# Second token block's output product in plain form, weight sums on VectorE instead of GpSimd, denser activation steps in the last turn

## The chip, the cores and the metric

The kernel runs on one core of one Trainium2 chip. The metric is device time in microseconds (us), lower is better. Verdicts use a margin of 2%. The engines are TensorE (PE in the profile; PEld is its weight load), VectorE (DVE), ScalarE (ACT), GpSimd (POOL) and SyncE (SP). PSUM is the memory in which TensorE's products are formed and from which VectorE or ScalarE takes them here; SBUF is the on-chip memory of the other operands. The granted clock is the share of TensorE's full clock that the profile shows. "TensorE stands" means that it is idle. One matmul of the program shows in the trace as two records; counts such as x5777 are records.

## The reference

A gated recurrence over 4 x 8 heads of 768 tokens with head size 48 gives a 3072 x 384 matrix; a feed-forward layer with the activation h * erf(softplus(h)) follows.

```python
f = 1.0 / (1.0 + np.exp(-f_logit))
for t in range(S):
    state = f[:, :, t, :, None] * state + np.einsum('bhd,bhe->bhde', k[:, :, t], v[:, :, t])
    y[:, :, t] = np.einsum('bhd,bhde->bhe', q[:, :, t], state)
x = y.transpose(0, 2, 1, 3).reshape(B * S, H * D)     # 3072 x 384
h = x @ w_in                                          # 384 -> 2048
g = h * erf(np.maximum(h, 0.0) + np.log1p(np.exp(-np.abs(h))))
return g @ w_out                                      # 2048 -> 384
```

## The kernel before

The 3072 tokens form 12 blocks of 256. The main loop has 12 turns (`it` from 0 to 11). In one turn TensorE works through a list of slots, one matmul each: the hidden product (`x @ w_in`) of one block and the output product (`g @ w_out`) of an earlier one. Between slots come the steps of the recurrence (`stage_d`, `stage_t`, `stage_s`, `stage_y`), the steps of the activation (`act_step`) and the steps of the block sums (`sum_step`). The program order on each engine is the order in which this loop emits the instructions.

The output product of a block comes in two forms. The plain one, `project_first`, was used for block 0 alone. The other, `project`, splits the matrices into 2 x 2 blocks and needs seven products of half size instead of eight. For that, VectorE must form sums of the hidden values (`sum_h`, 16 instructions a block), sums of `w_out` must have been formed once (`sum_w`, 16 instructions), and VectorE has to combine the seven products as they leave PSUM (`plus`).

```python
def activate(gr):                       # one group: 4 x 256 hidden values on 128 partitions
    e = epool.tile(...)                 # two buffers
    exp(e, h)                           # ScalarE, line 157
    yield
    for i in range(n):
        term(xs[i], h, i)               # ScalarE tanh, line 160; may load its table first
        yield
    for i in range(n):
        times(e, xs[i], i)              # VectorE, line 165
        yield
    ...
    nc.scalar.activation(out=e[:], in_=e[:], func=AF.Tanh, scale=SERF_C)      # line 559
    yield
    nc.vector.tensor_tensor(out=h, in0=h, in1=e[:], op=ALU.mult)              # line 561
    gr["done"] = True
...
def sum_w(gi):
    ...
    add(t[:, 0], b12, b11, ALU.subtract, nc.gpsimd)      # line 615, on GpSimd
    yield
    ... # three more
def sum_h(gr):
    while not gr["done"]:
        act_step()                      # line 636: steps forced, beside those placed by the slots
    ... # four adds on VectorE, line 615
def project_first(blk):
    ...  # the same `while` before each of the
         # 2 x 4 matmuls 128x384 per group, line 670; then
                    if j == FG - 1 and tt == CPB - 1:
                        to_sum.append(sum_w(gi))
...
def project(blk):
    ...  # matmuls 128x192, line 717 (718 in the changed kernel)
    def plus(out, x, y):                # line 725 (726 in the changed kernel)
        nc.vector.tensor_tensor(out=out, in0=x, in1=y, op=ALU.add)
    ...
def slots(it):
    ...
    if it == 2:
        return chain(*hiddens(3), project_first(0)), n_h + n_ft * CPB
    if it < n_blocks - 1:
        return chain(project(it - 2), *hiddens(it + 1)), n_o + n_h
    return chain(*[project(blk) for blk in range(n_blocks - 3, n_blocks)]), 3 * n_o
```

In the recurrence, `stage_d` is the decay product (TensorE, line 380), then two exponentials on ScalarE (`dp`, line 383, and `kd`, line 386), then two products on VectorE (`qd`, line 395, and line 399). `stage_y` is the product `y` (line 525). It writes into one of the two PSUM buffers that the transposes of `stage_t` also use, so it has to wait until the copy of `kT` (VectorE, line 422) has emptied one.

## Time and profile before

| | before |
|---|---|
| time, median of 4 runs with the changed kernel in the same rounds | 629.17 us (628.93 to 629.83) |
| span of the profiled run | 627.6 us |
| TensorE busy | 589.5 us, 94% |
| VectorE busy | 470.2 us, 75% |
| GpSimd busy | 38.4 us, 6% |
| waits of TensorE after 160 us | 5.9 + 3.8 + 1.1 + 1.0 + 0.4 us |

The table is read from the last row up: TensorE is the engine that must not stand, and after 160 us it stands for 12.2 us in five places (the sum of the last row). What GpSimd did at that time is seen in the groups of instructions of the kernel before, cut to GpSimd (line, engine, operation, names, shapes and count; then busy time and the mean of one in ns):

```profile
L615 POOL TENSOR_TENSOR wT<-w_out_sb 128x384 f32<-128x384 f32 x8 | 12.2, 1524 | 0.0
L615 POOL TENSOR_TENSOR wT<-w_out_sb,wT 128x384 f32<-128x384 f32 x8 | 11.2, 1396 | 3.8 <-PE ops L670 3.6
```

These 16 sums are 23.4 of GpSimd's 38.4 us. They are the part of the change that moves. (The program reuses its buffers, so names such as `wT`, `scratch` and `kn` in the views can also hold hidden values or sums.)

### The profile page before, as it was taken

The numbers are of one execution on the slowest core, as the hardware profiler recorded it, in microseconds if no ns is written. First come the engines' busy times: TensorE is split into PE (matmuls) and PEld (weight loads), VectorE is DVE, ScalarE is ACT, GpSimd is POOL, SyncE is SP. The second block draws the span as 40 slices with busy tenths as digits, with TensorE's granted clock in tenths as the row PEclk, the third lists the DMA queues.
The fourth block names the chain that finished last, engine by engine and source line by source line (L and its number), as shares of the span: only waits on it lengthen the run. The fifth ranks groups of instructions, "written<-read, shape, count | busy, mean of one in ns | idle before, by whom it ended". The sixth has DMA issues, their size and how long they took to land.

```text
span 627.6 us, 13891 instructions
## 1 busy us (share of the span) xinstructions
PE 589.5 (94%) x5777; PEld 524.7 (84%) x5777; DVE 470.2 (75%) x788; ACT 382.4 (61%) x483; POOL 38.4 (6%) x49
## 2 busy tenths in 40 slices
PE   8788699998976999999999999999999999999995
PEld 7567588887644988988998998998998989989995
DVE  4998998695589778678787876797887694756751
ACT  5725457978864457756675776765775656556200
POOL 1000011010176000000000000000000000000000
PEclk9879799999989899999999999999999999999999
DMA  9997743440321043043052052052030000000000
GB/s 200 247 241 215 216 123 63 88 78 12 63 56 26 1 78 76 1 79 75 4 102 52 2 102 51 3 102 52 3 76 14 2 27 1 19 8 1 25 26 29
DMA packets 155587, 41.35 MB, mean 66 GB/s; under 512 B 147328, under 2 KB 150400, under 8 KB 155520
## 3 DMA queue, kind: packets, MB, share of 16 engines
q1 hardware_dynamic: 153440, 40.02, 29.3%
q8 instruction: 47, 0.77, 0.5%
q10 hardware_dynamic: 2080, 0.39, 0.3%
q14 instruction: 20, 0.16, 0.1%
HBM read 35.59 MB, written 4.72 MB: 64 GB/s over the span
## 4 chain that ended last, share of the span: by engine, by line
PE 72%; DVE 12%; issue 6%; ACT 5%; DMA 2%; SPq 1%; POOL 1%; DVEq 0%; ACTq 0%; POOLq 0%
PE ops L717 31%; PE hps L587 29%; PE y L525 3%; PE ps_t L411 2%; PE ops L670 2%; PE ps_d L380 2%; DVE sv L438 1%; PE sc L460 1%; PE sc L468 1%; DVE sv L439 1%; DVE w_in_sb L322 1%; DMA qn<-in_q_dram 1%; DVE qA L496 1%; DVE w_in_sb L336 1%; ACT L160 1%
## 5 line engine op out<-in xcount | busy, mean ns | idle before, releaser
L587 PE MATMUL hps<-xT,w_in_sb 128*128 128x256 f32 x1152 | 264.7, 386 | 7.8 <-DVE w_in_sb L336 4.4
L587 PEld LDWEIGHTS hps<-xT,w_in_sb 128*128 128x128 f32 x1152 | 218.2, 192 | 41.2 <-DVE w_in_sb L336 3.4
L165 DVE SCALAR_TENSOR_TENSOR e<-x,e 128x1024 f32<-128x1024 f32 x96 | 120.2, 1252 | 13.5 <-ACT x L160 13.2
L160 ACT ACTIVATE x<-Hg,serf_bias 128x1024 f32<-128x1024 f32 x88 | 97.6, 1141 | 0.2
L157 ACT ACTIVATE e<-Hg 128x1024 f32<-128x1024 f32 x44 | 46.6, 1058 | 77.0 <-DVE Hg L561 73.2
L717 PE MATMUL ops<-wT,Hg 128*128 128x192 f32 x352 | 87.6, 331 | 0.0
L717 PE MATMUL ops<-wT,scratch 128*128 128x192 f32 x320 | 76.5, 331 | 5.9 <-DVE scratch L615 5.9
L717 PE MATMUL ops<-w_out_sb,Hg 128*128 128x192 f32 x352 | 72.6, 329 | 0.0
L561 DVE TENSOR_TENSOR Hg<-Hg,e 128x1024 f32<-128x1024 f32 x44 | 54.6, 1240 | 22.5 <-ACT e L559 22.4
L717 PEld LDWEIGHTS ops<-wT,Hg 128*128 128x128 f32 x352 | 62.1, 192 | 2.2
L594 ACT COPY Hg<-hps 128x1024 f32<-128x1024 f32 x44 | 44.4, 1010 | 31.0 <-PE hps L587 30.7
L717 PEld LDWEIGHTS ops<-w_out_sb,Hg 128*128 128x128 f32 x352 | 60.7, 192 | 2.6
L717 PEld LDWEIGHTS ops<-wT,scratch 128*128 128x128 f32 x320 | 57.0, 193 | 6.2 <-issue 6.2
L559 ACT ACTIVATE e<-e 128x1024 f32<-128x1024 f32 x48 | 50.4, 1050 | 6.4 <-DVE e L165 6.3
L496 DVE TENSOR_TENSOR qA<-sc,tri 64x256 f32<-64x256 f32 x68 | 28.7, 422 | 22.3 <-PE sc L468 21.3
L725 DVE TENSOR_TENSOR scratch<-scratch,ops 128x384 f32<-128x384 f32 (+1 forms) x44 | 22.2, 504 | 30.3 <-ACT scratch L733 25.0
L418 ACT COPY qA<-ps_t 64x512 f32<-64x512 f32 x48 | 27.7, 578 | 22.5 <-PE ps_t L411 20.6
L395 DVE TENSOR_TENSOR qd<-qn,dp 128x384 f32<-128x384 f32 x24 | 13.4, 556 | 35.6 <-ACT dp L383 34.4
L717 PE MATMUL ops<-w_out_sb,scratch 128*128 128x192 f32 x160 | 39.5, 328 | 0.0
L525 PEld LDWEIGHTS y<-qA,sv 128*32 128x32 f32 x1536 | 24.6, 113 | 17.2 <-issue 9.2
L525 PE MATMUL y<-qA,sv 128*32 128x64 f32 x1536 | 28.9, 226 | 9.3 <-issue 6.9
L438 DVE TENSOR_TENSOR sv<-sc,sv 48x192 f32<-48x192 f32 x80 | 28.4, 354 | 8.3 <-ACT qA L488 6.9
(109 smaller groups left out, 648.9 us busy)
## 6 DMA issues: line engine op xcount, KB each, us to landing
lt<-in_f_logit_dram SPq DMA_DIRECT2D x24, 192.0 KB, 3.8
qn<-in_q_dram SPq DMA_DIRECT2D x24, 192.0 KB, 3.3
out_dram<-scratch SPq DMA_DIRECT2D x12, 384.0 KB, 2.6
kn<-in_k_dram SPq DMA_DIRECT2D x23, 192.0 KB, 3.5
vt<-in_v_dram SPq DMA_DIRECT2D x23, 192.0 KB, 3.6
sv<-in_v_dram SPq DMA_DIRECT2D x84, 48.0 KB, 2.9
w_out_sb<-in_moe_w_in_dram SPq DMA_DIRECT2D x4, 768.0 KB, 6.3
Hg<-in_moe_w_in_dram SPq DMA_DIRECT2D x4, 768.0 KB, 6.4
```

Source lines behind the costliest of these rows:

```text
L157: nc.scalar.activation(out=dst[:], in_=h, func=AF.Exp)
L160: nc.scalar.activation(out=dst[:], in_=h, func=AF.Tanh, bias=serf_bias[:, i : i + 1], scale=SERF_KAB[i][0])
L165: nc.vector.scalar_tensor_tensor(out=e[:], in0=x[:], scalar=SERF_KAB[i][2], in1=e[:], op0=ALU.add, op1=ALU.mult)
L418: nc.scalar.copy(out=qAs[g][half(r), r], in_=pss[0][half(r)])
L438: nc.vector.tensor_tensor(out=new, in0=add, in1=old, op=ALU.add)
L496: nc.vector.tensor_tensor(out=qA[half(1 - r), r, :, half(c)], in0=sc[half(c), r], in1=tri1[half(c)].unsqueeze(1).broadcast_to((C, HP, C)), ...
L525: nc.tensor.matmul(y[M * i : M * (i + 1), kt, half(c)], lhsT=sv[:, r, c, a, o : o + M], rhs=qA[:, r, a, half(c)], start=(n == 0), stop=Tru ...
L559: nc.scalar.activation(out=e[:], in_=e[:], func=AF.Tanh, scale=SERF_C)
L561: nc.vector.tensor_tensor(out=h, in0=h, in1=e[:], op=ALU.mult)
L587: nc.tensor.matmul(hps[:, j, :], lhsT=w_in_sb[:, kt, ft * P : (ft + 1) * P], rhs=xTs[blk][:, kt, :], start=(kt == 0), stop=(kt == n_k - 1),)
L594: nc.scalar.copy(out=gr["h"], in_=hps[:])
L717: nc.tensor.matmul(place[n], lhsT=x[:, j, :], rhs=y, start=(gi == 0 and j == 0 and n in first), stop=(gi == n_g - 1 and j == 1), skip_grou ...
```

## The change

The intent: block 1's product becomes plain, so that it needs no block sums and cannot wait for them. `w_out`'s sums, now needed one turn later, go to VectorE, spread over every second slot of turns 2 and 3. The activation steps get a new spacing in turn 3 and a closer one in the last turn. The core of the diff, cut:

```diff
-        add(t[:, 0], b12, b11, ALU.subtract, nc.gpsimd)
+        add(t[:, 0], b12, b11, ALU.subtract)
 ... (the same for the other three)
-                        to_sum.append(sum_w(gi))
+                        if blk == 0:
+                            to_sum.append(sum_w(gi))
 ...
+        if it == 3:
+            return chain(project_first(1), *hiddens(4)), n_ft * CPB + n_h
 ...
-                at = ([0] if it + 2 == ADJACENT else []) + [2, 26, 42, 54, 76, 90]
+                at = [0, 1, 15, 24, 31, 52, 66] if it + 2 == ADJACENT else [2, 26, 42, 54, 76, 90]
 ...
+                elif it == 3:
+                    step = s % 7 in (1, 4)
+                elif it == n_blocks - 1:
+                    step = s % 3 == 1
                 else:
                     step = s % 9 in (2, 6)
 ...
                 if it == 2:
-                    if s == n - 6:
-                        to_sum.extend(sum_h(groups[1, gi]) for gi in range(NS))
-                    sum_step()
+                    if s % 2:
+                        sum_step()
 ...
-                    if s < n_o or s % 3 == 0 or it == n_blocks - 1:
+                    if it == 3:
+                        if s % 2:
+                            sum_step()
+                    elif s < n_o or s % 3 == 0 or it == n_blocks - 1:
                         sum_step()
```

More of the change, by code (lines that the diff above doesn't have):

```diff
@@ L602, in places @@
         own = [[sums_sb[:, b, n] for n in range(NA)] for b in range(NS)]
-        for _ in range((n_blocks - 3) * n_g // NS):
+        for _ in range((n_blocks - 4) * n_g // NS):
             yield from own
@@ L607, in places @@
             own.insert(0, [x[:, 0 : S_WORDS // (NS * NA)].rearrange("p (j t) -> p j t", j=FG // 2) for x in t])
-        own = own[1::-1] + own[3:] + own[2:3]
+        own = own[1::-1] + own[2:]
         while True:
@@ L612, with add @@
     sum_places = places()
-    def add(out, x, y, op=ALU.add, engine=nc.vector):
-        engine.tensor_tensor(out=out, in0=x, in1=y, op=op)
+    def add(out, x, y, op=ALU.add):
+        nc.vector.tensor_tensor(out=out, in0=x, in1=y, op=op)
     def sum_w(gi):
@@ L621, in sum_w @@
         t = w_sums(gi)
-        add(t[:, 0], b12, b11, ALU.subtract, nc.gpsimd)
+        add(t[:, 0], b12, b11, ALU.subtract)
         yield
-        add(t[:, 1], b22, t[:, 0], ALU.subtract, nc.gpsimd)
+        add(t[:, 1], b22, t[:, 0], ALU.subtract)
         yield
-        add(t[:, 2], b22, b12, ALU.subtract, nc.gpsimd)
+        add(t[:, 2], b22, b12, ALU.subtract)
         yield
-        add(t[:, 3], b21, t[:, 1], ALU.subtract, nc.gpsimd)
+        add(t[:, 3], b21, t[:, 1], ALU.subtract)
     def blocks(h):
@@ L963 @@
                 if it == 2:
-                    if s == n - 6:
-                        to_sum.extend(sum_h(groups[1, gi]) for gi in range(NS))
-                    sum_step()
+                    if s % 2:
+                        sum_step()
                 elif it > 2:
-                    if s == n_o and it < n_blocks - 1:
+                    if s == n - n_h and it < n_blocks - 1:
                         to_sum.extend(sum_h(groups[it - 1, gi]) for gi in range(NS))
```

## The prediction

> **What bounds the kernel now.** I read the engine table first, then the slices, then every wait of TensorE, then the three stretches in which TensorE stood.
>
> ```profile
> PE 589.5 (94%) x5777; PEld 524.7 (84%) x5777; DVE 470.2 (75%) x788; ACT 382.4 (61%) x483; POOL 38.4 (6%) x49
> ...
> PE   8788699998976999999999999999999999999995
> ...
> POOL 1000011010176000000000000000000000000000
> ```
>
> TensorE is the bound, but the PE row has a dent in slices 10 to 13 (15.7 us each, so 157 to 220 us), just where POOL has its only dense work. Busy time by stretch says the same:
>
> ```profile
> 160.00:180.00 20.00, 15.80 (x177) 10.71 (x175) 15.71 (x19) 14.27 (x20) 7.53 (x7) 0.95 0.15 26
> 180.00:204.00 24.00, 18.10 (x130) 12.09 (x123) 21.47 (x24) 13.70 (x16) 16.87 (x11) 0.93 0.25 51
> 204.00:236.00 32.00, 30.93 (x262) 28.81 (x262) 23.82 (x43) 17.22 (x21) 0.50 (x2) 0.93 0.22 40
> ...
> 280.00:566.00 286.00, 286.00 (x2728) 262.13 (x2727) 217.50 (x370) 188.12 (x214) 0.81 (x2) 1.00 0.19 38
> ```
>
> From 280 to 566 us TensorE is busy without a gap at full clock. So nothing saved on VectorE or ScalarE there is worth time; only TensorE's own work is. Between 160 and 280 it stands. Its waits from 160 to 240 us:
>
> ```profile
> PE ops L717 <- DVE scratch L615: 5.9, 1, 5.9
> PE y L525 <- issue: 3.8, 1, 3.8
> PE hps L587 <- DVE scratch L725: 1.1, 1, 1.1
> ```
>
> The first is block 1's product waiting for the block sums of its own hidden values. The second has no releaser named. VectorE's timeline gives it: y starts at 178.22 us, and the instruction that ends just before is the copy of kT out of the PSUM buffer (177.43 + 0.69 = 178.12). The changed program's wait list confirms that y of this chunk waits for that copy. The weight-load row of the same y is put down to POOL; I take that for the latest event, not the cause. What made the copy late is this:
>
> ```profile
> 172.03 1.29 DVE L439 TENSOR_TENSOR sv<-sv,Tall 48x192 f32<-48x192 f32 x1
> 173.33 1.93 DVE L165 SCALAR_TENSOR_TENSOR e<-x,e 128x1024 f32<-128x1024 f32 x1
> 175.28 0.35 DVE L438 TENSOR_TENSOR sv<-sc,sv 48x192 f32<-48x192 f32 x1
> 175.66 0.67 DVE L439 TENSOR_TENSOR sv<-sv,Tall 48x192 f32<-48x192 f32 x1
> 176.34 0.36 DVE L438 TENSOR_TENSOR sv<-sc,sv 48x192 f32<-48x192 f32 x1
> 176.73 0.67 DVE L439 TENSOR_TENSOR sv<-sv,Tall 48x192 f32<-48x192 f32 x1
> ```
>
> Elsewhere L439 takes 0.35 us and L165 1.22 us. They are stretched only while POOL runs w_out's sums (172.1 to 199 us), and only where both inputs lie in SBUF: L438, one of whose inputs is PSUM, keeps 0.35.
>
> **What the Trainium skill says.** "SBUF — State Buffer", section "Who interferes with whom": a VectorE instruction with two SBUF inputs and a GpSimd instruction that reads SBUF share one read interface, and the later one blocks for the other's whole instruction. The trace agrees on who suffers (L439 and L165, not L438). "GPSIMD Engine Reference", section 4.1: elementwise two-input work belongs on VectorE. The trace: POOL's 128x384 sums take 1.52 and 1.40 us; a VectorE tensor_tensor of the same shape and type (qd) takes 0.556. "TensorE: Matmul & The Clock Gate", section "What's actually happening": after an idle window of about 3.4 us the clock falls to half. The trace agrees: after the 5.9 us gap, 16 records of the 128x192 product run from 203.00 to 208.25 at 0.32 us instead of 0.1625, while after the 1.07 us gap at 230.6 us 18 records need 3.97 us (0.221 each against the usual 0.216), so nearly nothing.
>
> **The change part by part.**
>
> *Block 1's product plain instead of seven-product (TensorE).* Removed: 56 matmuls 128x192, two records each. At full clock 82 such records took 13.32 us on the chain, 0.1625 us each, so 112 are 18.20 us. Added: 32 matmuls 128x384, 64 records; 24 of them took 7.74 us, hence 0.3225 each, 0.325 with gaps: 20.8 us. Cost on the path: **+2.6 us**.
>
> *Block 1's sums vanish.* The wait of 5.90 us goes, since the plain product reads the hidden values themselves. So does the half-clock stretch behind it: 38 records in 9.24 us against 38 x 0.1625 = 6.18, so 3.06. Together **-9.0 us**. VectorE also loses 16 sums of about 0.44 (7.0 us) and the four PSUM combinations of block 1 (3 x 0.554 + 0.353 = 2.0 us); these lie beside TensorE.
>
> *w_out's 16 sums move to VectorE.* 16 x 0.556 = 8.9 us of VectorE work. In return the stretching stops: about 0.8 us on each of some 15 VectorE instructions, 12 us in all. VectorE is lighter on balance. On the path: no sum stands ahead of the late kT copy in the new order, so from 172.03 us the row of work is 0.35 + 1.15 + 4 x 0.37 + 0.7 = 3.7 and the copy ends near 175.75. y then starts at 175.85 rather than 178.22 (2.4 us). The remaining gap is 1.4 us (TensorE stopped at 174.45), too short for the clock to fall; in before y's 64 records and the first 12 of the product after it lost 0.95 and 0.76 us to it. Together **-4.0 us**.
>
> *VectorE releasing PSUM.* The hidden product at 231.62 waited 1.07 us for the last combination of block 1 (L725), which stood behind ScalarE's table load. The plain product is emptied by one ScalarE copy, and the buffer is needed only after 12 more matmuls: **-1.1 us**. The same wait recurs one turn later (0.98 us at 279.23). There the new order of ScalarE has dp's exponential some 1.5 us earlier by my reading of the order, so I count **-1.0 us**, less surely.
>
> *Act steps.* In turn 3 the number stays near 23 (104 x 2/9 before, 80 x 2/7 after). In the last turn they become denser. TensorE runs its 336 last records in 54.62 us, 0.1626 each, full rate: nothing to win, **0**.
>
> *New waits.* I laid the changed order out by hand with the durations above. The fourth group of block 0 has to be activated by about 183.6 us and comes at 183.3, so this is tight. The fourth group of block 1 comes at 203 and is needed at 207. Near the end of turn 3, the second y waits for ScalarE's qA copies behind an exponential that waits for VectorE: about 0.8 us. I count **+0.8 us**.
>
> Sum: 2.6 - 9.0 - 4.0 - 1.1 - 1.0 + 0 + 0.8 = -11.7 us; 628.98 - 11.7 = 617.3 us.
>
> **The rivals.**
>
> 1. VectorE becomes the wait: 16 sums land in the stretch where it is already 21.47 of 24.0 us busy, and TensorE then stands for the activation of block 0's last group or block 1's. For it: the 0.3 us margin. Against: that stretch contains the inflated durations, and every second slot leaves 1.3 us of plain product for each 0.5 us sum. If it holds, 3 to 6 us come back: 620 to 623.
> 2. The plain product costs more than its stalls: if the stalls merely move into the next turn, where block 2 is the first seven-product block and needs its sums, only the port contention is gained: 628.98 + 2.6 - 4.0 to -6 = 625 to 627.6. Against: block 2's sums are enqueued 48 hidden matmuls (20.7 us) before use and need 16 x 0.44 = 7 us.
> 3. Everything between 164 and 280 us falls shut, the new 0.8 us wait does not come and y's gap is halved: 615.8.
> 4. Denser activation in the last turn delays the PSUM combinations there. A buffer is released 16 matmuls (5.2 us) before reuse, so I give this under 1 us.
>
> **Range and chances.** Two per cent is 12.6 us, at 616.4 us. The estimate lies 0.9 us short of it, and the sum of all I see to gain is 12 to 13, so "faster" needs nearly every step to come whole: 0.3. Slower needs a new stall of over 24 us: 0.02. Low end 615.0 (rival 3 and a little), high end 621.5 (rival 1 in part).
>
> **What would show each step.** TensorE busy near 587 us, TensorE's two half-clock stretches gone (granted clock 1.00 from 170 to 230 us); POOL busy near 15 us; L439 at 0.35 and L165 at 1.22 throughout; no wait of TensorE on the sums (L615) of 5 us, y's gap near 175 us about 1.4 us; 64 more records of the plain product at 0.325 us and 112 fewer of the other. VectorE busy near 458 us. I am wrong if TensorE shows a new wait over 2 us on an activation (L561) or on block 2's sums, or if the last turn shows gaps.

## The result, and the profile after

The changed kernel took 619.63 us (median of 4 runs, 619.41 to 619.82) against 629.17. The ratio is 0.9847 with a 95% interval of 0.983 to 0.9864: 1.5% less, within the 2% margin. A ratio here is the mean time of one kernel's fast runs over that of the other's of the same rounds, so it is not quite the ratio of the medians quoted.

The engine table and the slices of the changed kernel (busy us and share, instructions; then busy tenths in 40 slices):

```profile
PE 588.2 (95%) x5729; PEld 515.0 (83%) x5729; DVE 460.4 (75%) x784; ACT 382.5 (62%) x483; POOL 15.5 (3%) x33
...
PE   8789699999999999999999999999999999999995
...
POOL 1000011010000000000000000000000000000000
```

The dent in the PE row is gone, and with it the only dense stretch of POOL. TensorE lost just 1.3 us of busy time; the rest of the gain is standing time. By stretch, in the order of the prediction's second view (start and end; length, then busy us and instructions of PE, PEld, DVE, ACT and POOL; granted clock, DMA share, GB/s):

```profile
160.00:180.00 20.00, 18.07 (x185) 11.65 (x184) 15.61 (x24) 16.61 (x22) 1.50 (x2) 1.00 0.17 28
180.00:204.00 24.00, 24.00 (x141) 14.37 (x140) 21.33 (x36) 13.51 (x16) 0.00 (x0) 1.00 0.22 46
...
270.00:556.00 286.00, 285.00 (x2724) 261.10 (x2723) 212.35 (x363) 187.19 (x214) 0.51 (x2) 1.00 0.19 38
```

From 180 to 204 us TensorE now has no gap, at clock 1.00 instead of 0.93. VectorE works 21.33 us there as against 21.47 before: it took in the sums, and what it took in, the stretching gave back. The last line is the surprise: the part that was without a gap before (286.00 of 286) now has one of 1.00 us. All waits of TensorE after 160 us (released by what; us in total, times, longest):

```profile
PE y L525 <- issue: 1.5, 1, 1.5
PE hps L587 <- DVE scratch L726: 1.0, 1, 1.0
PE ops L718 <- DVE scratch L726: 0.9, 1, 0.9
PE ops L670 <- ACT Hg L594: 0.4, 1, 0.4
```

12.2 us of waits have become 3.8. The second and third of these lines are new in place. VectorE's timeline ahead of `y` (start, length in us, engine, line, operation):

```profile
172.00 1.23 DVE L165 SCALAR_TENSOR_TENSOR e<-x,e 128x1024 f32<-128x1024 f32 x1
...
174.77 0.69 DVE L422 COPY kT<-ps_t 128x512 f32<-128x512 f32 x1
```

L165 is back at 1.23 us (1.93 before), and the copy of kT starts at 174.77 instead of 177.43.

To find where the time went, I compare the moments at which the same piece of work starts in both traces. The start-up before 160 us is the same code and still varied: over all 13 profiled runs block 0's product began between 163.64 and 164.77 us. The tail after that moment varied too: 7.1 us in the one trace of the changed kernel, 6.0 to 6.5 in the others. So I count from the first matmul of block 0's product (line 670) and stop at the start of VectorE's last row of combinations (line 725 or 726), and call this **the stretch**. It is 621.18 - 164.27 = 456.91 us before and 610.63 - 163.88 = 446.75 us after: 10.16 us less.

| piece of work | from the start of the stretch: before | after | gained in all | gained since the row above |
|---|---|---|---|---|
| y at 178.22 / 175.57 us | 13.95 | 11.69 | 2.26 | 2.26 |
| block 1's product | 28.24 | 24.77 | 3.47 | 1.21 |
| hidden product of turn 3 | 60.94 | 50.96 | 9.98 | 6.51 |
| output product of turn 4 | 86.06 | 74.77 | 11.29 | 1.31 |
| hidden product of turn 5 | 156.25 | 143.74 | 12.51 | 1.22 |
| hidden product of turn 7, at 413.28 / 401.62 us | 249.01 | 237.74 | 11.28 | -1.23 |
| last row of combinations | 456.91 | 446.75 | 10.16 | -1.12 |

Up to turn 5 the change gained 12.51 us. Then 2.35 us are given back: 1.23 between the hidden products of turns 5 and 7, where the trace shows one wait, in turn 6, and 1.12 after that, where it shows one in the last turn.

The loss in turn 6, in the timeline of the changed kernel, ScalarE and VectorE in order of time (in square brackets the idle time before, and what ended it):

```profile
353.68 1.06 ACT L157 ACTIVATE e<-Hg 128x1024 f32<-128x1024 f32 x1 [3.81 <-DVE Hg L561]
354.74 1.28 ACT L160 ACT_TABLE_LOAD   x1
...
357.09 0.47 ACT L383 ACTIVATE dp<-ps_d 128x384 f32<-128x384 f32 x1
357.60 0.56 DVE L395 TENSOR_TENSOR qd<-qn,dp 128x384 f32<-128x384 f32 x1 [2.81 <-ACT dp L383]
...
358.66 1.53 DVE L726 TENSOR_TENSOR scratch<-scratch,ops 128x384 f32<-128x384 f32 x3
```

This is read backwards. TensorE waits for the combinations (L726), whose PSUM buffer it wants. They stand behind `qd` (L395) in VectorE's row. `qd` waits for the decay exponential (L383) on ScalarE. That stands behind an activation exponential, a table load and a tanh, which themselves began late, after 3.81 us of waiting for VectorE. In the kernel before, the same row of instructions stands at 272.58 to 277.56 us, in turn 4, with the same durations. It was this that made TensorE wait 0.98 us at 279.23 us. In the changed kernel turn 4 has no such row: there the exponential of `dp` comes directly behind L157, and the combinations start 1.56 us after it (263.01 and 264.57 us).

The loss in the last turn, in the same view of the changed kernel:

```profile
573.92 1.22 DVE L561 TENSOR_TENSOR Hg<-Hg,e 128x1024 f32<-128x1024 f32 x1
...
576.19 1.52 DVE L726 TENSOR_TENSOR scratch<-scratch,ops 128x384 f32<-128x384 f32 x3
577.86 0.56 PE L718 MATMUL ops<-wT,scratch 128*128 128x192 f32 x2 [0.88 <-DVE scratch L726]
```

From 565 to 577.6 us VectorE stands for only 0.6 us there. Ahead of the three combinations stand twelve block sums of 0.42 us and, among them, one last product of the activation (L561). In the kernel before, the twelve sums stand ahead of the combinations too, but without an L561 among them, and TensorE does not wait.

### The profile page after: what moved, and what is told of

It reads as the page before. It is cut to its first block, busy times and chain, and to the rows that moved or that the text cites. A ratio compares the mean times of both kernels' runs of the same rounds, so it can differ in the third digit from the quotient of the medians.

```text
span 617.7 us, 13765 instructions
## 1 busy us (share of the span) xinstructions
PE 588.2 (95%) x5729; PEld 515.0 (83%) x5729; DVE 460.4 (75%) x784; ACT 382.5 (62%) x483; POOL 15.5 (3%) x33
## 4 chain that ended last, share of the span: by engine, by line
PE 73%; DVE 12%; ACT 7%; DMA 3%; issue 2%; SPq 1%; POOL 0%; DVEq 0%; ACTq 0%; POOLq 0%
PE hps L587 30%; PE ops L718 25%; PE ops L670 7%; PE y L525 3%; PE ps_t L411 3%; PE ps_d L380 2%; ACT x L160 2%; PE sc L468 1%; PE sc L460 1%; DVE sv L439 1%; DVE sv L438 1%; DMA Tall<-dp 1%; DVE Hg L561 1%; SPq L391 1%; DVE w_in_sb L336 1%
## 5 line engine op out<-in xcount | busy, mean ns | idle before, releaser
L165 DVE SCALAR_TENSOR_TENSOR e<-x,e 128x1024 f32<-128x1024 f32 x96 | 117.1, 1220 | 13.1 <-ACT x L160 12.6
L157 ACT ACTIVATE e<-Hg 128x1024 f32<-128x1024 f32 x44 | 46.5, 1058 | 61.8 <-DVE Hg L561 57.6
L718 PE MATMUL ops<-wT,Hg 128*128 128x192 f32 x320 | 78.9, 328 | 0.0
L561 DVE TENSOR_TENSOR Hg<-Hg,e 128x1024 f32<-128x1024 f32 x44 | 53.8, 1222 | 22.2 <-ACT e L559 21.9
L718 PE MATMUL ops<-wT,scratch 128*128 128x192 f32 x288 | 67.8, 326 | 0.9 <-DVE scratch L726 0.9
L718 PE MATMUL ops<-w_out_sb,Hg 128*128 128x192 f32 x320 | 65.1, 326 | 0.0
L594 ACT COPY Hg<-hps 128x1024 f32<-128x1024 f32 x44 | 44.4, 1010 | 32.7 <-PE hps L587 32.4
L718 PEld LDWEIGHTS ops<-wT,Hg 128*128 128x128 f32 x320 | 55.8, 190 | 1.9
L718 PEld LDWEIGHTS ops<-w_out_sb,Hg 128*128 128x128 f32 x320 | 54.6, 190 | 2.0
L718 PEld LDWEIGHTS ops<-wT,scratch 128*128 128x128 f32 x288 | 50.3, 190 | 1.1 <-issue 1.1
L726 DVE TENSOR_TENSOR scratch<-scratch,ops 128x384 f32<-128x384 f32 (+1 forms) x40 | 20.1, 503 | 31.8 <-ACT scratch L734 24.5
L395 DVE TENSOR_TENSOR qd<-qn,dp 128x384 f32<-128x384 f32 x24 | 13.4, 556 | 32.5 <-ACT dp L383 32.5
L718 PE MATMUL ops<-w_out_sb,scratch 128*128 128x192 f32 x144 | 35.2, 326 | 0.0
```

What stands on the lines that cost most here:

```text
L157: nc.scalar.activation(out=dst[:], in_=h, func=AF.Exp)
L165: nc.vector.scalar_tensor_tensor(out=e[:], in0=x[:], scalar=SERF_KAB[i][2], in1=e[:], op0=ALU.add, op1=ALU.mult)
L594: nc.scalar.copy(out=gr["h"], in_=hps[:])
L718: nc.tensor.matmul(place[n], lhsT=x[:, j, :], rhs=y, start=(gi == 0 and j == 0 and n in first), stop=(gi == n_g - 1 and j == 1), skip_grou ...
```

## The experiments

"After" means the changed kernel. The sum:

| run | stretch, us | timed median, us | ratio to before |
|---|---|---|---|
| before | 456.91 | 628.3 to 629.2 by batch | 1 |
| after | 446.75 | 619.63 | 0.9847 |
| a_w_sums_on_pool | 450.05 | 622.82 | 0.9907 |
| b_w_sums_on_vector | 449.44 | 621.53 | 0.9885 |
| a_third_block_plain | 449.18 | 621.63 | 0.9883 |
| a_sums_every_slot | 449.52 | 623.38 | 0.9916 |
| a_last_turn_as_before | 447.49 | 619.70 | 0.9855 |
| a_last_turn_denser | 448.08 | 620.06 | 0.9864 |
| a_decay_product_later | 453.68 | 627.23 | 0.9975 |
| a_decay_product_later2 | 445.51 | 618.27 | 0.9835 |
| a_decay_later_again | 445.51 | 617.62 | 0.9829 |
| a_both_waits | 444.40 | 616.98 | 0.9822 |
| b_decay_product_later | 454.30 | 626.10 | 0.9957 |

Each stretch is from one trace, so tenths of it are not to be leaned on; the two runs of one kernel (a_decay_product_later2 and a_decay_later_again) agree in it to 0.01 us, while their medians differ by 0.65. Against before, every run counts as "same" by the 2% margin; what follows compares medians and traces. Where two runs come from different batches, before itself differs by up to 0.9 us between them, and the ratio is the safer comparison.

### The sums back on GpSimd: a_w_sums_on_pool

After, with the four additions of `sum_w` on GpSimd again.

```diff
-        add(t[:, 0], b12, b11, ALU.subtract)
+        add(t[:, 0], b12, b11, ALU.subtract, nc.gpsimd)
 ... (the same for the other three)
```

> The changed kernel with w_out's 16 sums back on GpSimd (block 1's product stays plain). Theory (the port): VectorE's instructions with two SBUF inputs stretch again between 172 and 199 us (L165 near 2.0 us, L439 0.67 to 1.3), the kT copy ends near 178 instead of 175.5, y's gap grows from 1.5 to about 3.8 us and the clock falls after it: 4 us slower than the changed kernel, 623.6 us. No wait on block sums returns. Rival (the plain product does it all, the stretching lies beside TensorE): within 1 us of the changed kernel, 619 to 620.6.

Measured: 622.82 us (622.22 to 623.46), 3.2 us over after's 619.63; the stretch is 3.30 us longer. VectorE's timeline:

```profile
172.03 1.29 DVE L439 TENSOR_TENSOR sv<-sv,Tall 48x192 f32<-48x192 f32 x1
173.34 1.93 DVE L165 SCALAR_TENSOR_TENSOR e<-x,e 128x1024 f32<-128x1024 f32 x1
```

These are the lengths of the kernel before to the hundredth, in a program with another output product. The copy of kT is at 177.43 us again, `y` waits 3.8 us again. No wait on sums comes back. So the stretching and the gap before `y` belong to the sums on GpSimd and to nothing else in the change.

### The sums on VectorE and nothing else: b_w_sums_on_vector

Before, with the sums on VectorE in every slot.

```diff
-        add(t[:, 0], b12, b11, ALU.subtract, nc.gpsimd)
+        add(t[:, 0], b12, b11, ALU.subtract)
 ... (the same for the other three)
```

> The kernel before with w_out's 16 sums on VectorE in every slot (block 1 stays the seven-product form). Theory: y's gap shrinks as in the changed kernel (4 us), and VectorE reaches block 1's second group of sums near 196.6 us with TensorE arriving near 193, so that wait falls from 5.9 to about 3.6 us and the half-clock stretch behind it shrinks a little: 622 to 624 us. Rival 1 (VectorE has no room: 8.9 us of added sums push block 1's sums back as much as the end of the stretching pulled them forward): y's gap shrinks but the wait on sums grows to 9 us, 628 to 630. Rival 2 (the move to VectorE is the whole gain): 619.6 or less.

Measured: 621.53 us (620.28 to 623.57); the stretch is 7.47 us shorter than before's. The largest waits of TensorE, and the first matmuls behind the largest:

```profile
PE ops L717 <- DVE scratch L615: 2.7, 1, 2.7
PE hps L587 <- DVE scratch L725: 2.0, 2, 1.1
```

```profile
197.06 1.01 PE L717 MATMUL ops<-wT,scratch 128*128 128x192 f32 x2 [2.71 <-DVE scratch L615]
```

Without the stretching VectorE gets to block 1's sums sooner as well: their wait falls from 5.90 to 2.71 us though the product is still the seven-product one. The half clock behind it (the 2 records of this line take 1.01 us instead of 0.49) lasts 3.1 us from the restart, to 200.2 us, instead of 5.7 (203.0 to 208.7 us). So the two large parts of the change overlap. Without the plain product the stretch loses 7.47 us, without the move (the run above, 456.91 - 450.05) 6.86, and with all of it 10.16, not 14.33.

### The plain product one more time: a_third_block_plain

After, with block 2's product plain too, so that no wait is removed and the cost of the plain form stands alone.

```diff
+        if it == 4:
+            return chain(project_first(2), *hiddens(5)), n_ft * CPB + n_h
 ...
-                elif it == 3:
+                elif it in (3, 4):
                     step = s % 7 in (1, 4)
 ...
-                    if s == n - n_h and it < n_blocks - 1:
+                    if s == n - n_h and 3 < it < n_blocks - 1:
```

(The stages of the recurrence got turn 3's slots in turn 4, and the places of the sums one block's fewer.)

> The changed kernel with block 2's product plain too (32 matmuls 128x384 instead of 56 of 128x192, turn 4's slots scaled to 80 as turn 3's are, no block sums for block 2). There is no stall of TensorE in turn 4 of the changed kernel to remove. Theory: this costs what the records say, 64 x 0.325 minus 112 x 0.1625 = 2.6 us: 622.2 us, if the phase of the later activation steps makes no further difference (0 to 1.2 us either way, the wait on a PSUM combination in turn 6 may come or go). Rival: the plain form is really no dearer on the path, because its fewer weight loads and the lighter VectorE pay for it: 619.6 or less.

Measured: 621.63 us (620.49 to 622.27), 2.0 us over after by the medians; the stretch is 2.43 us longer. This is the price of the plain form, predicted at 2.6. The waits are as many and as long as in after, but the one on a combination has moved from turn 6 to turn 8 (the second line is a_sums_every_slot, the next run, where it falls in turn 7):

```profile
456.43 4.12 PE L587 MATMUL hps<-xT,w_in_sb 128*128 128x256 f32 x18 [0.98 <-DVE scratch L726]
409.64 4.12 PE L587 MATMUL hps<-xT,w_in_sb 128*128 128x256 f32 x18 [0.99 <-DVE scratch L726]
```

In turn 8 `qd` again stands for the decay exponential just ahead of the combinations, for 2.81 us, as in turn 6 of after. So the wait goes with the order of the instructions and not with a place in the program.

### Denser sums: a_sums_every_slot

After, with a sum in every slot of turns 2 and 3.

```diff
-                    if s % 2:
-                        sum_step()
+                    sum_step()
 ...
-                        if s % 2:
-                            sum_step()
+                        sum_step()
```

> The changed kernel with the sums of turns 2 and 3 in every slot instead of every second. Theory from the run that had them so in the kernel before: the only harm is that the activation of block 0's last group comes 0.43 us late for TensorE; so 0.4 to 0.8 us slower than the changed kernel, 620.0 to 620.4. Rival (the spacing in every second slot is what makes VectorE's room): waits over 2 us on an activation, 622 or more.

Measured: 623.38 us (621.39 to 623.78), 3.8 us over after by the medians; the stretch is 2.77 us longer. TensorE's waits have two new lines, of 2.0 us on ScalarE's copy of a hidden product and of 0.4 us on the activation of a group of block 0. The first is:

```profile
PE hps L587 <- ACT Hg L594: 2.0, 1, 2.0
```

I had expected 0.4 to 0.8 us, so the expectation missed and its rival came. The trace is that of the fastest of the four runs; the others took 623.2 to 623.8 us, and no trace shows what they lost beside. So the spacing is part of the gain: 2.4 us of waits come with the sums packed closer. The wait of 0.4 us (at 184.01 us) is VectorE's row: one more sum stands ahead of the L561 that TensorE waits for, which starts at 182.73 us instead of 182.11. The wait of 2.0 us is ScalarE's row: the copy of the hidden product (L594) stands behind an exponential and three tanh of the activation (223.87 to 227.95 us), and in after it stood ahead of the like, at 221.86. In the program order, block 2's sums are asked for earlier here and force the activations that they need into the row ahead of the copy (the `while` in `sum_h`).

### The last turn: a_last_turn_as_before and a_last_turn_denser

After, with the last turn's activation steps as in before:

```diff
-                elif it == n_blocks - 1:
-                    step = s % 3 == 1
```

> The changed kernel with the last turn's activation steps at the old rate (2 in 9 slots instead of 1 in 3). Theory: the 0.88 us wait of TensorE on a PSUM combination (L726) at 577.9 us comes from the denser steps, which put block 10's sums and an activation product ahead of it on VectorE; without them the last turn runs at 0.1626 us a record, 1.1 us faster, 618.5 us. Rival: the wait comes from something else that shifted (the phase of the turns before), and stays: 619.6, same within 0.3 us.

Measured: 619.70 us (619.66 to 620.04), no faster; my expectation missed. The wait of TensorE on the combinations is 1.60 us instead of 0.88. Among the twelve sums ahead of them now stand three instructions of the activation (two L165 and one L561), and a second L561 directly behind. So the denser steps alone did not make this wait; with them it is shorter. Nor are the activations late. From the last turn's first matmul (566.38 us before, 555.09 us here) the last three L561 start after 9.65, 21.44 and 25.30 us in the kernel before and after 7.58, 19.59 and 23.64 us here, at the same rate of steps. They come some 2 us earlier, and so one falls among the twelve sums that before stood behind the combinations. The theory of the next expectation, that they are a group behind, has this the wrong way round.

After, denser still:

```diff
-                    step = s % 3 == 1
+                    step = s % 2 == 1
```

> The changed kernel with activation steps in every second slot of the last turn instead of every third. New theory after the old rate did not help: TensorE's wait in the last turn comes because the activations are one group behind those of the kernel before, so that an activation product (L561, and at the old rate two L165 as well) stands among block 10's twelve sums and ahead of block 9's last three combinations; waits were 0 without, 0.88 us with one L561, 1.6 us with L165, L561, L165. Here the built order has no L561 or L165 among those sums, so the wait goes: 618.6 us, 1.0 us faster than the changed kernel. Rival: the first combination (pair 2), which now stands behind more activation work, comes too late instead and TensorE waits there: 619.6 or more.

Measured: 620.06 us (619.63 to 620.60), no faster; the expectation missed. TensorE waits 1.0 us for the combinations and 0.7 us for a block sum: steps that come sooner only change what stands in VectorE's row. That VectorE's row is what is too long here is tested below.

### The decay product three slots later: a_decay_product_later and a_decay_product_later2

Theory: the 1.0 us in turn 6 comes from the decay exponential standing between the table load and the combinations. If the decay product comes after the end of the output product, the combinations go ahead of `qd`. First try:

```diff
-                at = [0, 1, 15, 24, 31, 52, 66] if it + 2 == ADJACENT else [2, 26, 42, 54, 76, 90]
+                at = [0, 1, 15, 24, 31, 52, 66] if it + 2 == ADJACENT else [2, 26, 42, 57, 76, 90]
```

> The changed kernel with the decay product of the next chunk (ps_d and all that follows it) in slot 57 instead of 54 of turns 4 and later, so that VectorE's three last combinations of a block come ahead of qd and kd instead of behind them. Theory: the 1.0 us wait of TensorE on the last combination in turn 6 (360.3 us) is the wait that the kernel before had in turns 3 and 4, moved: VectorE stands for ScalarE's dp, which stands behind an exponential and a table load. With the new order that wait goes, 1 us or a little more faster: 618.5. Rival: the wait only moves elsewhere again, for instance to the transposition at slot 76, whose qd now comes later: 619.6 or slower, 620 to 621.

Measured: 627.23 us (625.54 to 628.59), 7.6 us worse by the medians. The waits of TensorE show why:

```profile
PE ps_d L380 <- ACT lt L365: 5.4, 5, 2.7
```

The preparation of the decays (`prepare`) is placed 14 slots ahead of the next decay product in the program, and so slid by three slots as well, from 40 to 43. TensorE then waited five times for its logarithm on ScalarE (line 365). The edit had moved two things. Second try, with the preparation left at slot 40:

```diff
+                at = [0, 1, 15, 24, 31, 52, 66] if it + 2 == ADJACENT else [2, 26, 42, 57, 76, 90]
 ...
-                prepare_at = at[todo.index((stage_d, (it + 3) * CPB))] - 14
+                prepare_at = at[todo.index((stage_d, (it + 3) * CPB))] - (17 if it + 2 > ADJACENT else 14)
```

> The same as the run with the decay product in slot 57, but with the preparation of its logarithms (table load, exponential, logarithm) left in slot 40, where the changed kernel has it. The first try let the preparation slide to slot 43 as well, and TensorE then waited 5.4 us in all for the logarithms. Theory: without that, VectorE's three last combinations come ahead of qd and kd, and the 1.0 us wait of turn 6 goes: 618.6 us. Rival: ps_d still waits for the logarithms or the transposition at slot 76 for qd: 619.6 to 622.

Measured: 618.27 us (617.10 to 618.69); the stretch is 1.24 us shorter. The wait in turn 6 is gone and no other came. (The medians, of two batches, differ by 1.4 us and the ratios by 0.0012, within their intervals; it is the trace that shows the gain.)

### The same edit alone in the kernel before: b_decay_product_later

This asks whether before's waits in turns 3 and 4 have the same cause, or whether a wait taken away there comes back later.

```diff
-                at = ([0] if it + 2 == ADJACENT else []) + [2, 26, 42, 54, 76, 90]
+                at = ([0] if it + 2 == ADJACENT else []) + [2, 26, 42, 57, 76, 90]
 ...
-                prepare_at = at[todo.index((stage_d, (it + 3) * CPB))] - 14
+                prepare_at = at[todo.index((stage_d, (it + 3) * CPB))] - (17 if it + 2 >= ADJACENT else 14)
```

> The kernel before with nothing but the decay product three slots later in every turn from the fourth on (preparation kept in its slot). Theory (the waits of TensorE on VectorE's last combination, 1.07 us in turn 3 and 0.98 us in turn 4, come from the table load and the decay exponential that stand between them on ScalarE and VectorE): both go, and the time is 2.0 us less than before, ratio 0.9968. Rival (TensorE runs ahead until it meets ScalarE's pace, so a wait removed in turns 3 and 4 comes back as a wait of about the same size in turn 5 or 6, as it did in the changed kernel): the time is less by under 0.7 us and the trace shows a wait on L725 or on an activation in a later turn.

Measured: 626.10 us (625.14 to 626.71), ratio 0.9957; the stretch is 2.61 us shorter. VectorE's timeline in turn 3:

```profile
225.89 1.53 DVE L725 TENSOR_TENSOR scratch<-scratch,ops 128x384 f32<-128x384 f32 x3
229.71 0.56 DVE L395 TENSOR_TENSOR qd<-qn,dp 128x384 f32<-128x384 f32 x1 [2.29 <-ACT dp L383]
```

The combinations now run 3.8 us ahead of `qd`. TensorE has no wait on them in any turn, and none has come back elsewhere. The rival falls. The waits come from the order of two instructions, not from TensorE running ahead of ScalarE's pace.

### Both later waits away: a_both_waits and a_decay_later_again

After with the edit of a_decay_product_later2, and with the next block's sums in the last turn put in the row later:

```diff
-                    if it == n_blocks - 1 and s % n_o == 40 and s < 2 * n_o:
+                    if it == n_blocks - 1 and s % n_o == 48 and s < 2 * n_o:
```

> The changed kernel with the decay product three slots later (and its preparation kept where it was), and in the last turn the block sums of the next block put in the row at slot 48 of 56 instead of 40, so that 8 sums and one last product of the activation stand ahead of the three PSUM combinations on VectorE instead of 12 and one. Theory (TensorE in the last turn waits 0.9 us because VectorE has too much in its row ahead of the combinations): four sums fewer are 4 x 0.42 = 1.7 us, more than the wait, so it goes; time 0.9 us under the run with the decay product later alone, 617.4 us, and no wait of TensorE over 0.5 us after 280 us. Rival (VectorE is late by work before this row, or the sums now come late for the next block): the wait moves to the block sums and the time is that of the decay product alone, 618.3 us.

> The same kernel as in the run a_decay_product_later2, again, as the partner of a_both_waits on the same chip. Expected 618.3 us as there, ratio to before 0.9835 within 0.002; wait of TensorE on VectorE's combination in turn 6 absent, the one in the last turn 0.9 us.

Measured, in the same rounds: 616.98 us (616.66 to 618.82), ratio 0.9822 (0.9803 to 0.9841), and 617.62 us (616.95 to 619.10), ratio 0.9829. All waits of TensorE after 160 us in a_both_waits:

```profile
PE y L525 <- issue: 1.5, 1, 1.5
PE ops L670 <- ACT Hg L594: 0.4, 1, 0.4
```

Both new waits are gone, and the stretch is 2.35 us shorter than after's, the very amount given back in the first table. By the timed runs the second edit alone is 0.64 us and lies within the scatter of both kernels; the trace (0.9 us of wait gone, 1.11 us of stretch) shows it, the medians do not settle it. This version has the lowest median and beats both kernels.

## Why the prediction was right or wrong

The time was right within its range: predicted 617.3 us (615.0 to 621.5), measured 619.63, and "within 2%" was the likeliest class. The sum was 11.7 us; in the stretch 10.16 came. That it came so near is in part luck: two terms fell 2.1 us short together (turn 4 and 6, and the last turn), and a feared wait of 0.8 us that did not come made up for part of it. By the prediction's own steps:

| step | predicted | measured in the stretch |
|---|---|---|
| y's gap and the clock behind it | -4.0 | -3.47 (3.30 when undone alone) |
| block 1's sums and half clock, with the plain product | -9.0 + 2.6 = -6.4 | -6.51 |
| PSUM wait in turn 3 | -1.1 | -1.31 |
| the same wait in turn 4 | -1.0 | -1.22 in turn 4, +1.23 in turn 6 |
| activation steps of the last turn | 0 | +1.12 from the last turn |
| new wait for the second `y` of turn 3 | +0.8 | 0 |
| sum | -11.7 | -10.16 |

**What held.** The stretching of VectorE by GpSimd and its cost are shown by putting the sums back: the same lengths and 3.2 us return. The plain product's own cost, 2.6 us, is shown at 2.0 (medians) to 2.4 us (traces) by doing it once more. Block 1's sums no longer appear among the waits. The counts came as said: VectorE 460.4 us busy (458 predicted), GpSimd 15.5 (15), TensorE 588.2 (587), and 5729 TensorE instructions, which is 5777 - 112 + 64.

**The step that failed: "I count -1.0 us, less surely".** The reason given was that "the new order of ScalarE has dp's exponential some 1.5 us earlier". That is true of turn 4, and the wait there did go. But I read the changed order no further than turns 3 and 4. Where the activation falls in a turn shifts from turn to turn, and in the changed kernel the same row (exponential, table load, tanh, decay exponential, `qd`, combinations) forms in turn 6. The gain of this term was 1.22 us and its loss 1.23, so it was worth nothing. The two runs with the decay product later show the cause, in both kernels.

What shifts the row is in the line "In turn 3 the number stays near 23". By a count in the two programs (not in a run), turn 3 places 23 activation steps by its slots in both. But the sums of block 2, which are asked for before its activation is done, force 6 more in the changed kernel (line 636) and 2 in the kernel before, so the activations that follow come up to 4 steps earlier in the order. In a_sums_every_slot 8 are forced, and in a_third_block_plain 5, one turn later. Following this count, the row forms wherever a turn begins at one and the same step of the activation: turns 3 and 4 before, 6 in after, 7 and 8 in those two runs. There the traces have the wait. (Turn 9 of the kernel before begins so too, but has no decay product at that slot.) No run takes the forced steps away alone, so this much is argued, not shown.

**The second step that failed: "nothing to win, 0", with rival 4, "under 1 us".** I reasoned from the last turn of the kernel before, where TensorE had no gap, and asked only what the denser steps could win or delay. The last turn lost 1.12 us, 0.88 of it a visible wait. Rival 4 had the engine, the wait and the size right and the sum left it out; and "if the last turn shows gaps" was the prediction's own sign of being wrong. Its cause, the denser steps, is not the whole one: at the old rate the wait is 1.60 us. What the traces show is that an activation product (L561) that stood behind the combinations before now stands ahead of them, among the block sums, because the activations come earlier: the last L561 starts 25.30 us after the turn's first matmul before and 19.20 us after it in the changed kernel, and 23.64 us at the old rate. a_both_waits shows that taking four sums out of that row removes the wait. That the forced steps of turn 3 make the activations earlier at the old rate is the likely source, by the count above; no run tests it alone.

**The new wait that did not come.** I laid out turn 3 by hand and found 0.8 us for the second `y`. In the trace that `y` starts at 230.92 us and TensorE has no gap there. The order was as I had laid it out: the exponential L157 at 228.62 us had waited 1.29 us for VectorE, and the copies `qA` stand behind it. But they end at 230.75 us, just as TensorE is through with the work ahead. So the row was right and its timing was not, and the term hid 0.8 of the 2.35 us lost.

**A size that was off.** Of the 4.0 us at `y`, 2.26 came as the earlier start (2.4 predicted) and 1.21 as faster work behind it (0.95 + 0.76 predicted). The granted clock is 1.00 from 175.5 us on, so the clock term did come. After `y`, though, the 36 records of the plain product from 176.71 to 188.65 us take 0.332 us each, against 0.323 for the 28 from 191.77 to 200.80 us: 0.3 us in all. Most of it is the activation that the prediction called tight, of block 0's last group, ended at 182.11 + 1.22 = 183.33 us and needed at once:

```profile
183.38 4.81 PEld L670 LDWEIGHTS ops<-w_out_sb,wT 128*128 128x128 f32 x16 [0.57 <-DVE wT L561]
```

The two records of TensorE there start 0.44 and 0.43 us after the one before, instead of 0.32; the rest, 0.1 us, lies at the first record after `y`.

The rivals: VectorE as the new wait (rival 1) came to no more than these 0.2 us with sums in every second slot. With sums in every slot 2.4 us of waits came, 0.4 of them on VectorE's activation and 2.0 on ScalarE's copy. The stalls did not move to block 2's sums (rival 2; by its own sum its lower end is 625.6 and not 625).

From the stretch to the clock on the wall, 10.16 us became 9.9 between the two traces and 9.54 between the medians. The single trace of the changed kernel has a tail 0.65 us longer than before's, and a start-up 0.39 us shorter; no other trace has such a tail, so I take these for scatter.

## What to carry to other kernels

When a change removes a wait of about a microsecond by shifting the order of two engines, look for the same row of instructions in every later turn: a wait that comes from order can reappear where the order falls the old way again, and steps that the program forces early shift that order for all that follows. Remove it by putting what releases the buffer ahead of what waits for another engine; three slots did that here and were worth 2.5 us even in the kernel before. Gains of two parts that shorten the same wait do not add, so run each alone before summing them, and when an edit of one position moves others that hang on it, pin those first.

## What the Trainium skill lacked or had wrong

- "TensorE: Matmul & The Clock Gate", section "What's actually happening", has the clock halve after at least one idle window of about 3.4 us. In b_w_sums_on_vector a gap of 2.71 us was enough: the granted clock was 0.50 from 197.0 to 200.0 us. Gaps of 1.52 us (after) and 1.07 us (before) left it at 1.00.
- "ScalarE: Activation LUTs", section "What ACT_TABLE_LOAD costs", gives 1283 ns for the load, which the trace confirms (1.28 us), and about 1380 ns more for a drain at every switch. No such drain is seen here: in the changed kernel L157 ends at 353.68 + 1.06 = 354.74 us, the load starts at 354.74, and the tanh behind it at 356.04, 0.02 us after the load's end. A switch cost 1.30 us on ScalarE, not 2.66.
